# Fused sliding-window attention and MLP: four PSUM banks for up-projections that run alone, scores issued beside value products, w_out in 8 KB runs

## The chip, the cores and the metric

The kernel runs on one core of a Trainium2 chip. The metric is the device time of one execution in microseconds. Three executions of the kernel before took 350.82, 351.66 and 353.08 us, so the median is 351.66 us.

## The reference

```python
def _attn_ref(q, k, v):                    # (8, 8, 576, 64) each: batch, heads, tokens, width
    scores = np.matmul(q, k.transpose(0, 1, 3, 2)) / 8
    rel = pos[:, None] - pos[None, :]
    scores = np.where((rel >= 0) & (rel < 64), scores, -1e9)
    ...                                    # softmax over the last axis
    return np.matmul(attn, v)

def _moe_ref(x, w_in, w_out):              # x: 4608 x 512, w_in: 512 x 2048, w_out: 2048 x 512
    h = x @ w_in
    g = h * (1.0 / (1.0 + np.exp(-1.702 * h)))
    return g @ w_out
```

Attention looks back 64 tokens. Its output, with the heads side by side, is the input of the MLP. The kernel computes in bf16 and adds up in fp32.

## The kernel before, in words

The 4608 tokens are cut in two ways. Attention goes by blocks m = 0 to 35 of 128 tokens; the MLP goes by chunks of 512 tokens, ch = 0 to 8, four blocks to a chunk.

One attention block is a line of small steps. `turn_pe` (L166) transposes q and k on TensorE into `qkt`; VectorE copies q out, ScalarE copies k out. Later batches are transposed by DMA instead (`turn_dma`, L110, on SP's queue). `scores` (L187) is 16 small matmuls into one PSUM tile; `exp` (L202, ScalarE) and `mask` (L206, VectorE) make the weights; `pv` (L215) is 16 small matmuls with the values; `norm` (L231, VectorE) divides. The result `xs` is transposed into `xT`, by TensorE and a ScalarE copy (`x_mm`, L253, `x_out`, L261) for the first three chunks, and by DMA (`x_dma`, L264) after that.

`up` (L271) makes one piece of the hidden layer: 16 matmuls of 128 moving columns, or 8 of 256, or 4 of 512, into one PSUM bank, then tanh on ScalarE (`th`) and one VectorE operation to `gT`. `down` (L292) is 4 matmuls of 512 columns into an output bank; four of them make 128 tokens of output, which `down_out` (L306) scales on ScalarE and ScalarE's own queue stores. So a chunk is 16 `up` pieces of equal work and 16 `down` pieces.

PSUM is eight banks: two for S (one tile of two banks), two for the tag T (one tile of two banks: the value products, or a transpose), two single banks for H (hidden pieces), two single banks for O (outputs, or transposes).

The order of work on every engine is the order of the program text; nothing is reordered. It has five stages:

1. Start, up to L342. Blocks 0 to 2 of batch 0 go through attention one after the other. `arrive` (L320) casts what has landed: q on VectorE, k on ScalarE, v on GpSimd. `warm` is idle matmuls of 512 columns. The weights are loaded from GpSimd's queue (`load_w_in`, `load_w_out`). At L345 a one-element GpSimd copy reads a part of w_out that is loaded third and writes the stage buffer that the next load takes: so SP's later loads start only when that part has landed.
2. Up-projection of chunk 0, L349 to L363: 16 calls of `up`, alone on TensorE but for block 3.
3. Down-projection of chunk 0, L366 to L386, with block 4 in between (L369 to L381).
4. Up-projection of chunk 1, L391 to L412: four rounds, each with one attention block (m + 1) and four calls of `up`.
5. From L461: slots 16 ch + i. Every slot is one `up` of chunk ch and one `down` of chunk ch - 1. Attention steps are hung into the slots by tables: `pe` between the two, `post` ahead of the slot. There `scores(m)` stands in slot `slot_s[m]`, its exp one slot later, mask and `pv(m)` two slots later.

Of the kernel before, what the change touches and what calls it, by code (L numbers as in the profile page):

```python
# [1 line left out]

# [26 lines left out]
def kernel(  # L29
# [14 lines left out]
    xs_pool = ctx.enter_context(tc.tile_pool(name="xs", bufs=3))  # L44
    rc_pool = ctx.enter_context(tc.tile_pool(name="rc", bufs=2))
    xt_pool = ctx.enter_context(tc.tile_pool(name="xt", bufs=2))
    th_pool = ctx.enter_context(tc.tile_pool(name="th", bufs=2))
    gt_pool = ctx.enter_context(tc.tile_pool(name="gt", bufs=8))
    ob_pool = ctx.enter_context(tc.tile_pool(name="ob", bufs=4))
    psS = ctx.enter_context(tc.tile_pool(name="psS", bufs=1, space=bass.MemoryType.PSUM))  # L50
# [67 lines left out]
    def load_w_in(j):  # L118
        f = slice(512 * j, 512 * j + 512)
        nc.gpsimd.dma_start(  # L120
            out=w_in_sb[:, :, f], in_=moe_w_in.rearrange("(c p) f -> p c f", p=P)[:, :, f]
        )

    def load_w_out(j):
        f = slice(4 * j, 4 * j + 4)
        nc.gpsimd.dma_start(
            out=w_out_sb[:, f, :], in_=moe_w_out.rearrange("(c p) d -> p c d", p=P)[:, f, :]
        )


# [35 lines left out]
    def turn_pe(pool, tag, b, i):  # L166
        n = size(i)
        ps = pool.tile([P, 8, P], bf16, name="turn", tag=tag)
        for w in range(2):
            for hp in range(4):  # L170
                nc.tensor.transpose(  # L171
                    out=ps[:, 4 * w + hp, 0:n],
                    in_=rows[b % 2][w][0:n, i, P * hp : P * hp + P],
                    identity=ident[0:n, 0:n],
                )
        for w, op in enumerate((nc.vector.tensor_copy, nc.scalar.copy)):
            op(  # L177
                out=qkt[b % 2][:, w::2, PAD + P * i : PAD + P * i + n],
                in_=ps[:, 4 * w : 4 * w + 4, 0:n],
            )  # L180
# [20 lines left out]

    def exp(m):  # L202
        E_of[m] = ep_pool.tile([P, 2, 512], bf16, name="E", tag="E")
        nc.scalar.activation(out=E_of[m][:], in_=S_of.pop(m)[:], func=AF.Exp, scale=scale)  # L204

    def mask(m):  # L206
        z = next((t for t, b, j in blocks_of(m) if j == 0), None)
        pt = PT_of[m] = ep_pool.tile([P, 2, 512], bf16, name="PT", tag="PT")
        nc.vector.tensor_tensor(  # L209
            out=pt[:].rearrange("p a f -> p (a f)"),  # L210
            in0=E_of.pop(m)[:].rearrange("p a f -> p (a f)"),
            in1=masks[z][:].rearrange("p a t g c -> p (a t g c)"),
            op=ALU.mult,
        )
# [31 lines left out]
    def x_dst(m):  # L246
        ch = m // 4
        if m % 4 == 0:
            how = "pe" if ch < 3 else "dma"
            xT[ch] = xt_pool.tile([P, 4, 512], bf16, name=f"xT_{how}", tag=f"xT_{how}")  # L250
        return xT[ch][:, :, (m % 4) * P : (m % 4) * P + P]

# [13 lines left out]


    gT = {}
    H_of, O_of = {}, {}

    def up(ch, f, nf, t0, nt):  # L271

        ps = psH.tile([P, nf, nt], fp32, name="hps", tag="H")
        for g in range(nf):
            for c in range(4):
                nc.tensor.matmul(  # L276
                    ps[:, g, :],
                    lhsT=w_in_sb[:, c, (f + g) * P : (f + g + 1) * P],
                    rhs=xT[ch][:, c, t0 : t0 + nt],
                    start=(c == 0),  # L280
                    stop=(c == 3),
                )
        th = th_pool.tile([P, nf, nt], bf16, name="th", tag="th")
        nc.scalar.activation(out=th[:], in_=ps[:], func=AF.Tanh, scale=0.851)  # L284
        if (ch, f // 4) not in gT:
            gT[ch, f // 4] = gt_pool.tile([P, 4, 512], bf16, name="gT", tag="gT")
        nc.vector.scalar_tensor_tensor(  # L287
            out=gT[ch, f // 4][:, f % 4 : f % 4 + nf, t0 : t0 + nt],
            in0=th[:], scalar=1.0, in1=ps[:], op0=ALU.add, op1=ALU.mult,
        )  # L290

    def down(ch, i):  # L292

# [12 lines left out]
    def down_out(ch, tsub):  # L306
        o_sb = ob_pool.tile([P, DM], fp32, name="o_sb", tag="o_sb")
        nc.scalar.activation(out=o_sb[:], in_=O_of.pop((ch, tsub))[:], func=AF.Copy, scale=0.5)  # L308
        nc.scalar.dma_start(out=out_tiled[:, ch * 4 + tsub, :], in_=o_sb[:])

    def warm(n):
        ps = psH.tile([P, 512], fp32, name="idle", tag="H")
# [14 lines left out]
    exp(0)  # L327
    for m in range(3):
        arrive(0, m + 1)
        if m == 1:  # L330
            for j in range(4):
                load_w_in(j)
        mask(m)
        pv(m)
        norm(m)
        turn_pe(psO, "O", 0, m + 1)
        x_mm(m, psO, "O")
        x_out(m)
        scores(m + 1)
        exp(m + 1)  # L340
        if m < 2:
            warm(4)  # L342
    for j in range(4):
        load_w_out(j)
    nc.gpsimd.tensor_copy(out=stage[5][0:1, 0, 0:1], in_=w_out_sb[0:1, 8, 0:1])  # L345
    load_f32(0, 4)
    for i in range(5):
        load_f32(1, i)
    up(0, 0, 4, 0, P)  # L349
    up(0, 0, 4, P, P)  # L350
    mask(3)
    pv(3)
    norm(3)
    up(0, 0, 4, 2 * P, P)
    up(0, 4, 4, 0, P)
    x_mm(3, psO, "O")
    x_out(3)
    up(0, 4, 4, P, P)
    up(0, 4, 4, 2 * P, P)
    up(0, 0, 4, 3 * P, P)  # L360
    up(0, 4, 4, 3 * P, P)
    for f in range(8, 16):
        up(0, f, 1, 0, 512)  # L363


    for i in range(16):  # L366
        if i % 4 == 0 and i > 0:
            down_out(0, i // 4 - 1)
        if i == 10:  # L369
            arrive(0, 4)  # L370
            arrive(1, 0)
            turn_pe(psH, "H", 0, 4)
            turn_pe(psH, "H", 1, 0)
# [12 lines left out]
    down_out(0, 3)  # L386


    b2 = iter([lambda i=i: load_f32(2, i) for i in range(5)])
    next(b2)()  # L390
    for m in range(4, 8):  # L391
        scores(m + 1)
        exp(m + 1)
        t0 = (m % 4) * P
        up(1, 0, 4, t0, P)
        up(1, 4, 4, t0, P)
        mask(m + 1)
        pv(m + 1)
        norm(m + 1)
        if m < 7:  # L400
            arrive(1, m - 2)
        next(b2)()
        if m >= 6:
            cast_qk(2, m - 6, (nc.gpsimd, nc.gpsimd))
            turn_dma(2, m - 6)
            cast_v(2, m - 6)
        up(1, 8, 4, t0, P)
        x_mm(m + 1, psO, "O")
        x_out(m + 1)
        if m < 7:  # L410
            turn_pe(psO, "O", 1, m - 2)
        up(1, 12, 4, t0, P)  # L412

# [8 lines left out]
    def later(slot, g):  # L424
        post.setdefault(slot, []).append(g)

    slot_s = {9: 32, 10: 36, 11: 40, 12: 43, 13: 46}
    for m in range(14, NM):
        slot_s[m] = max(slot_s[m - 1] + 3, 4 * (m - 4) - 2)
    slot_pv = {m: s + 2 for m, s in slot_s.items()}  # L430

    for m in range(9, NM):
        if m < 12:
            at(slot_pv[m] + 1, lambda m=m: x_mm(m, psT, "T"), [lambda m=m: x_out(m)])
    for m in range(9, NM):
        at(slot_s[m], lambda m=m: scores(m), [lambda m=m: exp(m)])
        later(slot_pv[m], lambda m=m: mask(m))
        at(slot_pv[m], lambda m=m: pv(m), [lambda m=m: norm(m)])
        if m >= 12:
            later(slot_pv[m] + 1, lambda m=m: x_dma(m))  # L440

    for i in range(2, 5):
        at(32 + 2 * (i - 2), lambda i=i: cast_qk(2, i, (nc.gpsimd, nc.gpsimd)))
        at(32 + 2 * (i - 2), lambda i=i: turn_dma(2, i))
        at(32 + 2 * (i - 2), lambda i=i: cast_v(2, i))
    for b in range(3, B):
        free = slot_pv.get((9 * (b - 1) - 1) // 2, 31) + 2
        for i in range(5):
            use = slot_s[(S * b + P * i) // P]
            at(max(free, 38) + i, lambda b=b, i=i: load_bf16(b, i))  # L450
            at(use - 5, lambda b=b, i=i: turn_dma(b, i))
            at(use - 5, lambda b=b, i=i: shift_v(b, i))

    def unit(ch, i):
        if ch < 4:
# [54 lines left out]
```

## Time and profile before

| | |
|---|---|
| median of three runs | 351.66 us |
| the profiled execution | 355.03 us, of which the span is 353.3 us |
| TensorE | 310.0 us busy, 88% of the span |
| VectorE, ScalarE, GpSimd | 46%, 45%, 38% |
| DMA | mean 124 GB/s; in tenths by 40 slices 9999899946499999799999999993343331110021 |
| granted TensorE clock | mean 0.985 |

The profile shows the profiled execution alone. [...] The idle time beside a record is the engine's idle time before it and what ended it.

### The profile page before, as it was taken

To read this page: it belongs to the slowest core of one execution; us is meant where nothing else is said; L and a number is where in the kernel's file an instruction comes from. 1 tells how busy PE (TensorE), PEld (TensorE's weight loads), DVE (VectorE), ACT (ScalarE), POOL (GpSimd) and SP (SyncE) were. 2 spreads that over 40 slices of the span, in tenths; PEclk is the share of its full clock that TensorE was granted. 3 is DMA by queue.
4 is the path that set the end of the run, shared out by engine and by line. 5 is a ranking of instruction groups with operands and counts; after the bars stand their busy time and mean duration, and the time that the engine had idled before them with its cause. 6 is when DMAs were issued, how large, how long until landed. Compare 5 with 4: busy or idle time off the path is not lost.

```text
span 353.3 us, 7859 instructions
## 1 busy us (share of the span) xinstructions
PE 310.0 (88%) x3240; PEld 187.1 (53%) x3240; DVE 163.4 (46%) x285; ACT 158.0 (45%) x249; POOL 133.5 (38%) x190
## 2 busy tenths in 40 slices
PE   2777897677789996999999999999999999999995
PEld 1447343466666664676665665665444444444442
DVE  4535531456554453545445545544545544533400
ACT  3463424555444443444454454444445444444421
POOL 3670043745398589234983923492000000000000
PEclk9998999998899999999999999999999999999999
DMA  9999899946499999799999999993343331110021
GB/s 171 187 182 204 153 202 243 237 95 121 84 121 139 148 158 135 80 132 168 148 117 163 185 148 143 126 113 77 87 94 87 79 76 45 46 59 31 32 75 73
DMA packets 164579, 43.83 MB, mean 124 GB/s; under 512 B 155840, under 2 KB 159936, under 8 KB 164544
## 3 DMA queue, kind: packets, MB, share of 16 engines
q0 software_dynamic: 74544, 13.05, 53.5%
q1 hardware_dynamic: 84816, 20.85, 36.0%
q10 hardware_dynamic: 5184, 9.44, 7.4%
q8 instruction: 25, 0.41, 0.5%
q14 instruction: 10, 0.08, 0.1%
HBM read 36.70 MB, written 9.44 MB: 131 GB/s over the span
## 4 chain that ended last, share of the span: by engine, by line
PE 60%; DVE 17%; ACT 12%; DMA 6%; issue 2%; ACTq 1%; SPq 0%
PE ops L298 26%; PE hps L276 26%; DVE gT L287 8%; ACT th L284 7%; DVE PT L209 6%; PE Tacc L223 4%; DMA xT_dma<-xs 4%; PE S L194 3%; DMA stage<-in_k_dram 3%; ACT E L204 2%; DVE xs L236 2%; ACT o_sb L308 1%; ACT qkt L177 1%; PE turn L171 1%; DVE qkt L177 1%
## 5 line engine op out<-in xcount | busy, mean ns | idle before, releaser
L287 DVE SCALAR_TENSOR_TENSOR gT<-th,hps 128x512 bf16<-128x512 bf16 x144 | 98.9, 687 | 142.4 <-ACT th L284 142.0
L284 ACT ACTIVATE th<-hps 128x512 bf16<-128x512 f32 x144 | 85.9, 597 | 143.2 <-PE hps L276 131.1
L298 PE MATMUL ops<-w_out_sb,gT 128*128 128x512 bf16 x576 | 143.8, 380 | 0.0
L276 PEld LDWEIGHTS <-w_in_sb 128*128 128x128 bf16 x1376 | 102.9, 100 | 51.9 <-issue 6.0
L276 PE MATMUL hps<-xT_dma,w_in_sb 128*128 128x128 bf16 (+2 forms) x704 | 99.4, 282 | 3.1 <-DMA xT_dma<-xs 3.1
L298 PEld LDWEIGHTS <-gT 128*128 128x128 bf16 x576 | 51.2, 98 | 51.5
L276 PE MATMUL hps<-xT_pe,w_in_sb 128*128 128x128 bf16 (+1 forms) x672 | 52.9, 235 | 2.4 <-DVE gT L287 2.1
L102 POOL DMA_DIRECT2D v_nat<-in_v_dram x25 | 21.5, 860 | 43.7 <-issue 42.5
L204 ACT ACTIVATE E<-S 128x1024 bf16<-128x1024 f32 x36 | 36.7, 1020 | 2.1 <-PE S L194 1.6
L308 ACT ACTIVATE o_sb<-ops 128x512 f32<-128x512 f32 x36 | 21.5, 598 | 25.5 <-PE ops L298 25.4
L223 PEld LDWEIGHTS <-PT 128*64 128x64 bf16 x576 | 12.6, 114 | 33.5 <-DVE PT L209 33.4
L223 PE MATMUL Tacc<-v_nat,PT 128*64 128x65 bf16 x256 | 14.8, 202 | 12.5 <-DVE PT L209 12.5
L236 DVE TENSOR_TENSOR xs<-Tacc,rc 128x512 bf16<-128x512 f32 x36 | 24.9, 691 | 1.2
L223 PE MATMUL Tacc<-v_off,PT 128*64 128x65 bf16 x320 | 16.6, 201 | 9.6 <-DVE PT L209 9.6
L209 DVE TENSOR_TENSOR PT<-E,mask_None 128x1024 bf16<-128x1024 bf16 x28 | 20.3, 725 | 4.2 <-ACT E L204 4.2
L101 POOL DMA_DIRECT2D rows_k<-in_k_dram x25 | 21.6, 863 | 0.0
L101 POOL DMA_DIRECT2D rows_q<-in_q_dram x25 | 21.4, 856 | 0.0
L86 POOL CAST v_off<-stage 64x512 bf16<-64x512 f32 x15 | 9.1, 610 | 26.7 <-DMA stage<-in_v_dram 26.6
L194 PE MATMUL S<-qkt 64*128 64x64 bf16 x576 | 16.0, 196 | 3.6 <-ACT qkt L177 3.5
L106 POOL COPY v_off<-v_nat 64x528 bf16<-64x528 bf16 x25 | 16.8, 676 | 6.0 <-DMA v_nat<-in_v_dram 5.0
L194 PEld LDWEIGHTS <-qkt 64*128 64x128 bf16 x576 | 11.2, 98 | 12.0 <-issue 5.7
L108 POOL COPY v_off<-v_nat 64x528 bf16<-64x528 bf16 x20 | 13.7, 684 | 1.2
(39 smaller groups left out, 106.8 us busy)
## 6 DMA issues: line engine op xcount, KB each, us to landing
out_dram<-o_sb ACTq DMA_DIRECT2D x36, 256.0 KB, 2.5
stage<-in_q_dram SPq DMA_DIRECT2D x12, 256.0 KB, 5.1
stage<-in_k_dram SPq DMA_DIRECT2D x12, 256.0 KB, 5.1
stage<-in_v_dram SPq DMA_DIRECT2D x12, 256.0 KB, 5.2
rows_q<-in_q_dram POOLq DMA_DIRECT2D x20, 128.0 KB, 5.4
rows_k<-in_k_dram POOLq DMA_DIRECT2D x20, 128.0 KB, 6.0
v_nat<-in_v_dram POOLq DMA_DIRECT2D x20, 128.0 KB, 5.2
w_in_sb<-in_moe_w_in_dram POOLq DMA_DIRECT2D x4, 512.0 KB, 10.5
```

The costliest lines, as they stand in the source:

```text
L101: nc.gpsimd.dma_start(out=heads(rows[b % 2][w][0:n, i, :]), in_=rows_of(src, b, i))
L102: nc.gpsimd.dma_start(out=v_nat[b % 2][0:n, i, :, 0:D], in_=rows_of(v, b, i))
L194: nc.tensor.matmul(st[:, h % 2, t * 256 + hp * 64 : t * 256 + hp * 64 + 64], lhsT=src[part, 2 * hp + 1, 64 * j : 64 * j + 128], rhs=src[pa ...
L204: nc.scalar.activation(out=E_of[m][:], in_=S_of.pop(m)[:], func=AF.Exp, scale=scale)
L209: nc.vector.tensor_tensor(out=pt[:].rearrange("p a f -> p (a f)"), in0=E_of.pop(m)[:].rearrange("p a f -> p (a f)"), in1=masks[z][:].rearr ...
L223: nc.tensor.matmul(acc[t * 64 : t * 64 + 64, h // 4, (h % 4) * 66 : (h % 4) * 66 + 65], lhsT=pt[:, epos : epos + 64], rhs=win, start=True, ...
L236: nc.vector.tensor_tensor(out=xs[:].rearrange("p (b h d) -> p b h d", b=2, h=4), in0=view[:, :, :, 0:D], in1=rc[:].to_broadcast([P, 2, 4, D]),
L276: nc.tensor.matmul(ps[:, g, :], lhsT=w_in_sb[:, c, (f + g) * P : (f + g + 1) * P], rhs=xT[ch][:, c, t0 : t0 + nt], start=(c == 0), stop=(c ...
L284: nc.scalar.activation(out=th[:], in_=ps[:], func=AF.Tanh, scale=0.851)
L287: nc.vector.scalar_tensor_tensor(out=gT[ch, f // 4][:, f % 4 : f % 4 + nf, t0 : t0 + nt], in0=th[:], scalar=1.0, in1=ps[:], op0=ALU.add, o ...
L298: nc.tensor.matmul(O_of[ch, tsub][:, :], lhsT=gT[ch, j][:, f, tsub * P : (tsub + 1) * P], rhs=w_out_sb[:, 4 * j + f, :], start=(j == 0 and ...
L308: nc.scalar.activation(out=o_sb[:], in_=O_of.pop((ch, tsub))[:], func=AF.Copy, scale=0.5)
```

## The change

The diff does these things.

- `up` is split into its matmuls, its tanh and its VectorE step. With `wide=True` every second piece takes a bank of O in place of one of H. Stages 2 and 4 use this.
- The loops of stages 1 to 4 are put in another order. In stage 1 the transposes of the next block stand ahead of mask and pv, the idle matmuls are dealt in twos, and six stand ahead of stage 2. In stage 4 a round begins with the transposes, and `scores` follows the first piece.
- Chunk 0 and 1 store their outputs from SP's queue. Blocks 1 to 4 of batch 1 are cast by GpSimd alone. Chunk 3 gets `xT` through TensorE. The first quarter of w_in is loaded one block earlier.
- In stage 5, `scores(m+1)` stands in the slot of `pv(m)`; exp follows one slot later, mask two, and `pv(m+1)` at least three slots later, but for block 9. The slots of `pv` from block 9 on stay as they were. The later batches' loads are spread over three slots each, and `x_dma` stands one slot later.
- w_out is read so that a partition takes four neighbouring rows of 2 KB. That deals the features to partitions in fours, and `up` takes its weights with a step of four columns to match.

```diff
-    th_pool = ctx.enter_context(tc.tile_pool(name="th", bufs=2))
+    th_pool = ctx.enter_context(tc.tile_pool(name="th", bufs=3))
...
-            out=w_out_sb[:, f, :], in_=moe_w_out.rearrange("(c p) d -> p c d", p=P)[:, f, :]
+            out=w_out_sb[:, f, :],
+            in_=moe_w_out[512 * j : 512 * j + 512, :].rearrange("(p c) d -> p c d", c=4),
...
-            how = "pe" if ch < 3 else "dma"
+            how = "pe" if ch < 4 else "dma"
...
-    def up(ch, f, nf, t0, nt):
-        ps = psH.tile([P, nf, nt], fp32, name="hps", tag="H")
+    def up_mm(ch, f, nf, t0, nt, wide=False):
+        pool, tag = (psO, "O") if wide and next(turns) % 2 else (psH, "H")
+        ps = pool.tile([P, nf, nt], fp32, name="hps", tag=tag)
+        f0 = 512 * (f // 4)
...
-                    lhsT=w_in_sb[:, c, (f + g) * P : (f + g + 1) * P],
+                    lhsT=w_in_sb[:, c, f0 + (f + g) % 4 : f0 + 512 : 4],
...
+    def up(*args, **kw):
+        up_g(*up_th(*up_mm(*args, **kw)))
...
-        nc.scalar.dma_start(out=out_tiled[:, ch * 4 + tsub, :], in_=o_sb[:])
+        eng = nc.sync if ch < 2 else nc.scalar
+        eng.dma_start(out=out_tiled[:, ch * 4 + tsub, :], in_=o_sb[:])
...
+    GG = (nc.gpsimd, nc.gpsimd)
...
     for m in range(3):
         arrive(0, m + 1)
-        if m == 1:
-            for j in range(4):
+        if m == 0:
+            load_w_in(0)
+        elif m == 1:
+            for j in range(1, 4):
                 load_w_in(j)
+        turn_pe(psO, "O", 0, m + 1)
         mask(m)
         pv(m)
         norm(m)
-        turn_pe(psO, "O", 0, m + 1)
+        warm(2)
+        scores(m + 1)
+        exp(m + 1)
+        warm(2)
         x_mm(m, psO, "O")
         x_out(m)
-        scores(m + 1)
-        exp(m + 1)
-        if m < 2:
-            warm(4)
...
-    up(0, 0, 4, 0, P)
-    up(0, 0, 4, P, P)
+    warm(6)
     mask(3)
+    up(0, 0, 4, 0, P, wide=True)
     pv(3)
     norm(3)
...
-        if i == 10:
+        if i == 9:
             arrive(0, 4)
             arrive(1, 0)
...
-            arrive(1, 1)
+            arrive(1, 1, GG)
         down(0, i)
+        if i == 14:
+            x_mm(4, psT, "T")
+            x_out(4)
...
     for m in range(4, 8):
+        t0 = (m % 4) * P
+        turn_pe(psT, "T", 1, m - 3)
+        u = up_mm(1, 0, 4, t0, P, wide=True)
         scores(m + 1)
+        u = up_th(*u)
         exp(m + 1)
-        t0 = (m % 4) * P
-        up(1, 0, 4, t0, P)
-        up(1, 4, 4, t0, P)
+        up_g(*u)
+        u = [up_mm(1, f, 4, t0, P, wide=True) for f in (4, 8)]
+        u = [up_th(*x) for x in u]
         mask(m + 1)
         pv(m + 1)
+        up_g(*u[0])
         norm(m + 1)
+        up_g(*u[1])
         if m < 7:
-            arrive(1, m - 2)
+            arrive(1, m - 2, GG)
...
-        up(1, 8, 4, t0, P)
-        x_mm(m + 1, psO, "O")
+        up(1, 12, 4, t0, P, wide=True)
+        x_mm(m + 1, psT, "T")
         x_out(m + 1)
-        if m < 7:
-            turn_pe(psO, "O", 1, m - 2)
-        up(1, 12, 4, t0, P)
...
-    slot_s = {9: 32, 10: 36, 11: 40, 12: 43, 13: 46}
...
+    slot_pv = {8: 32, 9: 34, 10: 38, 11: 42, 12: 45}
+    for m in range(13, NM):
+        slot_pv[m] = max(slot_pv[m - 1] + 3, 4 * (m - 4) - 2)
+    for m in range(8, NM):
+        s = slot_pv[m]
+        if m + 1 < NM:
+            at(s, lambda m=m: scores(m + 1), [lambda m=m: exp(m + 1)])
+            later(s + 2, lambda m=m: mask(m + 1))
+        if m > 8:
+            at(s, lambda m=m: pv(m), [lambda m=m: norm(m)])
+            if m < 16:
+                at(s + 1, lambda m=m: x_mm(m, psT, "T"), [lambda m=m: x_out(m)])
+            else:
+                later(s + 2, lambda m=m: x_dma(m))
...
-            use = slot_s[(S * b + P * i) // P]
-            at(max(free, 38) + i, lambda b=b, i=i: load_bf16(b, i))
-            at(use - 5, lambda b=b, i=i: turn_dma(b, i))
+            use = slot_pv[(S * b + P * i) // P - 1]
+            come = max(free, 36) + 3 * i
+            at(come, lambda b=b, i=i: load_bf16(b, i))
+            at(max(use - 5, come + 4), lambda b=b, i=i: turn_dma(b, i))
```

## Rows read from the trace of the kernel before

**Rows 1.** Busy time by stage: busy us (x instructions) per engine, then clock, DMA share, GB/s.
```profile
0.00:24.13 24.13, 13.23 (x164) 7.80 (x165) 11.22 (x30) 10.20 (x15) 15.03 (x29) 1.00 1.08 177
24.13:46.19 22.06, 17.97 (x186) 12.58 (x181) 11.28 (x18) 10.46 (x18) 1.73 (x4) 0.92 1.07 186
46.19:64.38 18.19, 16.12 (x113) 7.50 (x112) 4.51 (x10) 6.07 (x10) 7.44 (x12) 1.00 1.09 218
64.38:100.39 36.01, 25.78 (x438) 22.23 (x436) 19.60 (x34) 19.01 (x33) 20.05 (x31) 0.91 0.66 125
100.39:138.90 38.51, 33.70 (x476) 23.92 (x476) 18.92 (x30) 18.42 (x29) 31.66 (x41) 1.00 1.84 142
138.90:353.30 214.40, 203.16 (x1872) 113.09 (x1872) 97.81 (x164) 93.84 (x146) 57.59 (x76) 1.00 0.84 100
```
**Rows 2.** Groups of instructions by line and shape: busy us, mean ns of one, idle before.
```profile
L276 PEld LDWEIGHTS <-w_in_sb 128*128 128x128 bf16 x1376 | 102.9, 100 | 51.9 <-issue 6.0 <-DMA xT_dma<-xs 3.2 <-DVE gT L287 0.2
L276 PE MATMUL hps<-xT_pe,w_in_sb 128*128 128x128 bf16 x640 | 44.8, 228 | 0.8 <-DVE gT L287 0.4
L204 ACT ACTIVATE E<-S 128x1024 bf16<-128x1024 f32 x36 | 36.7, 1020 | 2.1 <-PE S L194 1.6 <-ACT o_sb L308 0.4
L236 DVE TENSOR_TENSOR xs<-Tacc,rc 128x512 bf16<-128x512 f32 x36 | 24.9, 691 | 1.2
L209 DVE TENSOR_TENSOR PT<-E,mask_None 128x1024 bf16<-128x1024 bf16 x28 | 20.3, 725 | 4.2 <-ACT E L204 4.2
L276 PE MATMUL hps<-xT_dma,w_in_sb 128*128 128x128 bf16 x256 | 16.9, 219 | 2.7 <-DMA xT_dma<-xs 2.7
L177 ACT COPY qkt<-turn 128x512 bf16<-128x512 bf16 x8 | 4.7, 586 | 11.0 <-DVE qkt L177 11.0
L177 DVE COPY qkt<-turn 128x512 bf16<-128x512 bf16 x8 | 3.4, 422 | 4.9 <-PE turn L171 4.9
```
**Rows 3.** Timeline of TensorE, weight loads and matmuls: start us, us, what, idle before.
```profile
101.38 0.29 PEld L194 LDWEIGHTS <-qkt 64*128 64x128 bf16 x16
102.60 1.06 PE L276 MATMUL hps<-xT_pe,w_in_sb 128*128 128x128 bf16 x16
103.49 1.03 PE L298 MATMUL ops<-w_out_sb,gT 128*128 128x512 bf16 x4
```
**Rows 4.** Timeline of ScalarE in the start stage, columns as in Rows 3.
```profile
19.17 1.02 ACT L204 ACTIVATE E<-S 128x1024 bf16<-128x1024 f32 x1 [0.28 <-PE S L194]
20.09 0.61 ACT L95 CAST rows_k<-stage 128x512 bf16<-128x512 f32 x1
...
24.30 1.02 ACT L204 ACTIVATE E<-S 128x1024 bf16<-128x1024 f32 x1
```
**Rows 5.** Timeline of TensorE in the up-projection of chunk 0.
```profile
39.48 2.01 PE L276 MATMUL hps<-xT_pe,w_in_sb 128*128 128x512 bf16 x8 [0.41 <-DVE gT L287]
```
**Rows 6.** Timeline of ScalarE, its queue, and TensorE in the down-projection of chunk 0.
```profile
53.30 0.60 ACT L308 ACTIVATE o_sb<-ops 128x512 f32<-128x512 f32 x1 [2.85 <-PE ops L298]
56.16 0.34 ACTq L309 DMA_DIRECT2D out_dram<-o_sb  x1
...
57.21 0.29 PE L171 MATMUL turn<-ident,rows_k 64*128 64x64 bf16 x4 [2.00 <-ACT rows_k L95]
```
**Rows 7.** Timeline of GpSimd: the one-element copy behind the third w_out load.
```profile
39.35 0.18 POOL L345 CAST stage<-w_out_sb 1x1 f32<-1x1 bf16 x1 [14.89 <-DMA w_out_sb<-in_moe_w_out_dram]
```
**Rows 8.** Waits of TensorE from 64.38 to 100.39: total us, times, longest.
```profile
PE Tacc L223 <- DVE PT L209: 8.7, 4, 2.3
```
**Rows 9.** Waits of TensorE from 100.39 to the end: total us, times, longest.
```profile
PE Tacc L223 <- DVE PT L209: 9.0, 26, 0.8
PE hps L276 <- DMA xT_dma<-xs: 3.1, 2, 2.7
```
**Rows 10.** Timeline of TensorE where a value product waits for its mask.
```profile
104.36 1.06 PE L276 MATMUL hps<-xT_pe,w_in_sb 128*128 128x128 bf16 x16
106.00 0.22 PE L223 MATMUL Tacc<-v_off,PT 128*64 128x65 bf16 x1 [0.59 <-DVE PT L209]
```

More of the change, by code (lines that the diff above doesn't have):

```diff
@@ L1 @@
+import itertools
 from contextlib import ExitStack
@@ L268 @@
     gT = {}
-    H_of, O_of = {}, {}
-    def up(ch, f, nf, t0, nt):
-        ps = psH.tile([P, nf, nt], fp32, name="hps", tag="H")
+    O_of = {}
+    turns = itertools.count()
+    def up_mm(ch, f, nf, t0, nt, wide=False):
+        pool, tag = (psO, "O") if wide and next(turns) % 2 else (psH, "H")
+        ps = pool.tile([P, nf, nt], fp32, name="hps", tag=tag)
+        f0 = 512 * (f // 4)
         for g in range(nf):
@@ L282, in up, with up_th, up_g @@
                 )
+        return ps, ch, f, nf, t0, nt
+    def up_th(ps, ch, f, nf, t0, nt):
         th = th_pool.tile([P, nf, nt], bf16, name="th", tag="th")
         nc.scalar.activation(out=th[:], in_=ps[:], func=AF.Tanh, scale=0.851)
+        return th, ps, ch, f, nf, t0, nt
+    def up_g(th, ps, ch, f, nf, t0, nt):
         if (ch, f // 4) not in gT:
@@ L348 @@
         load_f32(1, i)
-    up(0, 0, 4, 0, P)
-    up(0, 0, 4, P, P)
+    warm(6)
     mask(3)
+    up(0, 0, 4, 0, P, wide=True)
     pv(3)
     norm(3)
-    up(0, 0, 4, 2 * P, P)
-    up(0, 4, 4, 0, P)
-    x_mm(3, psO, "O")
+    up(0, 0, 4, P, P, wide=True)
+    up(0, 0, 4, 2 * P, P, wide=True)
+    x_mm(3, psT, "T")
     x_out(3)
[L358 to L361, printed above, removed]
+    up(0, 4, 4, 0, P, wide=True)
+    up(0, 4, 4, P, P, wide=True)
+    up(0, 0, 4, 3 * P, P, wide=True)
+    up(0, 4, 4, 2 * P, P, wide=True)
+    up(0, 4, 4, 3 * P, P, wide=True)
     for f in range(8, 16):
-        up(0, f, 1, 0, 512)
+        up(0, f, 1, 0, 512, wide=True)
     for i in range(16):
@@ L373 @@
             turn_pe(psH, "H", 1, 0)
-        if i == 11:
+        if i == 10:
             scores(4)
@@ L380 @@
             norm(4)
-            arrive(1, 1)
+            arrive(1, 1, GG)
         down(0, i)
-    x_mm(4, psH, "H")
-    x_out(4)
-    turn_pe(psH, "H", 1, 1)
+        if i == 14:
+            x_mm(4, psT, "T")
+            x_out(4)
     down_out(0, 3)
-    b2 = iter([lambda i=i: load_f32(2, i) for i in range(5)])
-    next(b2)()
     for m in range(4, 8):
+        t0 = (m % 4) * P
+        turn_pe(psT, "T", 1, m - 3)
+        u = up_mm(1, 0, 4, t0, P, wide=True)
         scores(m + 1)
+        u = up_th(*u)
         exp(m + 1)
-        t0 = (m % 4) * P
-        up(1, 0, 4, t0, P)
-        up(1, 4, 4, t0, P)
+        up_g(*u)
+        u = [up_mm(1, f, 4, t0, P, wide=True) for f in (4, 8)]
+        u = [up_th(*x) for x in u]
         mask(m + 1)
         pv(m + 1)
+        up_g(*u[0])
         norm(m + 1)
+        up_g(*u[1])
         if m < 7:
-            arrive(1, m - 2)
-        next(b2)()
+            arrive(1, m - 2, GG)
+        load_f32(2, m - 4)
         if m >= 6:
-            cast_qk(2, m - 6, (nc.gpsimd, nc.gpsimd))
+            cast_qk(2, m - 6, GG)
             turn_dma(2, m - 6)
             cast_v(2, m - 6)
-        up(1, 8, 4, t0, P)
-        x_mm(m + 1, psO, "O")
+        up(1, 12, 4, t0, P, wide=True)
+        x_mm(m + 1, psT, "T")
         x_out(m + 1)
-        if m < 7:
-            turn_pe(psO, "O", 1, m - 2)
-        up(1, 12, 4, t0, P)
     pe = {}
@@ L425, in later @@
         post.setdefault(slot, []).append(g)
-    slot_s = {9: 32, 10: 36, 11: 40, 12: 43, 13: 46}
[L428 to L440, printed above, removed]
+    slot_pv = {8: 32, 9: 34, 10: 38, 11: 42, 12: 45}
[12 more added lines that the diff above has]
+                later(s + 2, lambda m=m: x_dma(m))
+    at(32, lambda: load_f32(2, 4))
     for i in range(2, 5):
-        at(32 + 2 * (i - 2), lambda i=i: cast_qk(2, i, (nc.gpsimd, nc.gpsimd)))
-        at(32 + 2 * (i - 2), lambda i=i: turn_dma(2, i))
-        at(32 + 2 * (i - 2), lambda i=i: cast_v(2, i))
+        at(4 * i + 24, lambda i=i: cast_qk(2, i, GG))
+        at(4 * i + 24, lambda i=i: turn_dma(2, i))
+        at(4 * i + 24, lambda i=i: cast_v(2, i))
     for b in range(3, B):
@@ L448 @@
         for i in range(5):
-            use = slot_s[(S * b + P * i) // P]
-            at(max(free, 38) + i, lambda b=b, i=i: load_bf16(b, i))
-            at(use - 5, lambda b=b, i=i: turn_dma(b, i))
-            at(use - 5, lambda b=b, i=i: shift_v(b, i))
+            use = slot_pv[(S * b + P * i) // P - 1]
+            come = max(free, 36) + 3 * i
+            at(come, lambda b=b, i=i: load_bf16(b, i))
+            at(max(use - 5, come + 4), lambda b=b, i=i: turn_dma(b, i))
+            at(max(use - 5, come + 4), lambda b=b, i=i: shift_v(b, i))
     def unit(ch, i):
```

## The prediction, on record before the result

> **What bounds the kernel now.** I read the page's shares first (TensorE 88% busy), then the table by stage, then the waits of TensorE in each stage. The table [rows 1] cuts the span at the first matmul of each stage: start, up of chunk 0, down of chunk 0, up of chunk 1, and the merged slots in two pieces. In the merged stage TensorE is busy 237 of 253 us; ahead of it, 73 of 100 us. So the kernel is bound by TensorE's order of work: its matmuls, and the places where it waits for a short chain on other engines. DMA is full until 64 us (shares 1.07 to 1.09 in the first three stages) and not after; ScalarE and VectorE are nowhere over 55%.
>
> A piece, `up` or `down`, costs TensorE 0.87 to 0.89 us at full clock: 0.89 from a start of `up` to the next `down` [rows 3], 16 matmuls at a pitch of 55.6 ns. [...]
>
> **Start and up of chunk 0 (0 to 46.19 us).** Before, one round of the start lasts 24.30 - 19.17 = 5.13 us from exp to exp [rows 4]. In the new order the key cast still stands behind exp on ScalarE (20.09, just as exp ends), the transposes behind the cast, and now mask waits on VectorE behind the copy that waits for those transposes. My chain for a round: exp 1.02, `x_out` 0.59 (now between exp and the cast), cast 0.61, key transposes 0.45, copy 0.42, mask 0.73, pv 0.55, two idle matmuls 0.86, scores 0.5, the sum 5.73, and some 0.08 for each of seven handoffs: 6.3 us. (Durations: [rows 2, 4]; the matmul steps are estimates from the pitch at half clock.) So the start gets slower, by some 1.1 us in each of two rounds. The last scores end near 26.6 instead of 24.1; then eight idle matmuls (some 0.22 each) and a transpose bring the first `up` to 28.5. From there 16 pieces at 0.89, plus 0.4 for pv, 0.2 for the transpose and 0.4 for the handover to the output banks, are 15.2 us. Before, the stage took 22.06: pairs of pieces wait 0.41 for a bank [rows 5], pv waits for mask, and the clock is at 0.92. Four banks end the first: ScalarE and VectorE are busy 10.5 and 11.3 us in the stage [rows 1], at most 0.7 us a piece, which fits within 0.89, and a bank has four pieces' time to come free. The stage ends at 43.8 to 44 instead of 46.19: **-2.2 us**. Bounds: -5 if the new start is no slower than the old, +2 if every handoff costs double and the clock starts low.
>
> **Down of chunk 0 (18.19 us).** ScalarE finishes an output at 53.90 and gets its store off at 56.16; only then come the key casts, and TensorE stands 2.00 us [rows 6]. With the stores on SP's queue ScalarE is free for the casts, and they stand one piece earlier. On SP each store waits for its ScalarE copy; behind it are loads and transposes of batch 2, which nobody needs for over 10 us. New: 16 pieces at 0.87, transposes 0.9, scores, pv and `x_mm` 1.0, and 0.3 of switches: 16.1 us, **-2.1 us**. What hides the rest: the third w_out part lands at 39.35 [rows 7], so the fourth should be there by 43 and is needed near 46.5; batch 1's first tile is needed at 52. If this cover is gone, the loads pace the stage and the gain is nothing. The longer runs of w_out I cost at nothing, as the wait for them ends ahead of their use; the bound is one or two us either way.
>
> **Up of chunk 1 (36.01 us).** Here pv waits 8.7 us in four rounds [rows 8], and a round is 9.0 us for 3.6 us of `up`. In the new order a round is still one chain, since T has one buffer, passed from transposes to pv to `x_mm`: transposes 0.45, copies 0.42 and 0.59 one after the other, scores 0.35, exp 1.02, mask 0.73, pv 0.40, norm 0.69, `x_mm` 0.22, `x_out` 0.59 [rows 2], the matmul steps by the pitch. That is 5.46, with handoffs and norm's short reciprocal 1.3 more: 6.8 us. The four `up` pieces lie beside it, two of them under exp and mask. Four rounds are 27.2; I add 1.0 for stretches at the lower clock, as this stage shows 0.91 now. So 28.2 instead of 36.0: **-7.8 us**. GpSimd takes eight casts of some 0.6 us more, as long as ScalarE's of the same shape [rows 4]; two tiles of five casts are at most 6 us of work in a round of 6.8, so it stays under the chain. The moved casts cost TensorE nothing then; if GpSimd fell behind, a round would become 7 to 8 us. Bounds: -12 (rounds of 6), -3 (rounds of 8).
>
> **Merged slots (252.9 us).** pv waits 9.0 us for its mask, 26 times [rows 9]. A wait of 0.59 delays pv by 104.36 + 0.89 to 106.00, that is 0.75 [rows 10], so up to 0.16 more than the idle shown; I take half, 2.1 in all. With mask two slots behind scores and pv a third slot later, a slot (1.74 us) lies between mask and its use. Only block 9 keeps the old distance. Chunk 3's transpose by DMA was late by 2.7 us; by TensorE it is there in time, for four times 0.22. The other wait of that kind (0.4) may grow by 0.6, since the slots before it get shorter and the DMA does not. So -9.0 - 2.1 - 2.7 + 0.9 + 0.6 + 0.4 (block 9): **-11.9 us**. Late next: norm ahead of `x_mm`, some tenths three times. Bounds: -15 (the switch between shapes is also saved, once per block), -7 (transposes of later batches, whose loads now start later, arrive late twice). The third `th` buffer and the spread loads I cost at nothing; the slack of ScalarE and the DMA share of 0.84 hide them, and without that cover they are in these bounds.
>
> **The strided weights** belong to all 1376 loads of `up`. No row of before has one. The nearest rows: loads of 128 contiguous columns stand 98 ns in the records, but 16 of them start within 0.29 - 0.10 us, one per 13 ns, or 26 ns for each of the two row groups [rows 3]. A piece of 128 columns needs one per 55.6 ns, so a load may take twice as long and cost nothing. Lower end: 0 (a stride cannot make it faster). Upper end: loads that don't overlap at all follow at their mean of 100 ns [rows 2]; 640 + 256 matmuls of 128 columns are then 44 ns later each: +39.8 us. Pieces of 256 and 512 columns hide 100 ns. I take 0, the row of 26 ns being of the same operation.
>
> [...]
>
> **The sum.** -2.2 - 2.1 - 7.8 - 11.9 = -24.0 us from the profiled execution's 355.03: 331.0. That execution is 1.0% above the median of 351.66, so I scale by 351.66 / 355.03: **328 us**.
>
> **Rivals.**
> (a) *The strided load sets the pitch of the 128-column pieces.* For it: no such load in the trace, and the loads of w_in are back to back with the matmuls. Against: the 26 ns. It decides from 55.6 + 24.0 / 896 = 82 ns per load; at 100 ns the time is 328 + 39 = 367 us, slower than before. At 70 to 80 ns it would eat most of the gain. 13%, most of it slower.
> (b) *The first 64 us are paced by DMA.* For it: shares over 1.0, and the same bytes. Against: TensorE waits there name casts and banks, not loads. Then the 4.3 us of the first two stages are lost: 332 us. 12%.
> (c) *The stage of chunk 1 keeps its length*, because its chain gets new waits (T's one buffer, GpSimd's casts) or TensorE falls to the lower clock in the gaps. For it: the stage shows 0.91 now. Against: 8.7 us of its waits have one cause that is moved. 328 + 7.8 = 336 us. 13%.
> (d) *The merged slots get nothing*: the wait for mask turns into one for the next transpose. 340 us. 6%.
>
> **How the numbers follow.** My forecast has 56%, and its own range is 319 to 336. The best ends of the four stages (-5, -3, -12, -15) give 317; the worst (+2, 0, -3, -7) give 343, which also holds (b), (c) and (d). I take 317 to 345; outside are (a) and a little beyond. A measurement of this kernel can tell about 1% from no change. Faster by more than that: all but (a) and a pile of worst ends, 83%; within: 6%; slower: 11%.
>
> **What would show it.** Right: pv no longer waits for mask after the first merged slots; a round of stage four lasts about 6.8 us; up pieces of chunk 0 follow at 0.89 us; 16 matmuls of 128 columns still take 0.89 us from `up` to the next piece. Wrong: a longer pitch there (a); a first `up` well ahead of or behind 28.5 us; TensorE waiting for `rows` or `qkt` in the stage of chunk 1; waits for `xT_dma` or `qkt` of several us in the merged slots.

## The result, and the profile after

The changed kernel takes 327.95 us in the median of four runs (327.28 to 329.68), the kernel before 352.37 us beside it: a ratio of 0.9328, with a 95% interval of 0.9267 to 0.939. The forecast was 328. In the profiled executions the span falls from 353.3 to 326.8 us, by 26.5 us.

The table of the changed kernel by the same five stages: the start, up of chunk 0, down of chunk 0, up of chunk 1, merged slots (busy us and instructions of PE, PEld, DVE, ACT and POOL, then clock, DMA share, GB/s). The clock of 1.00 in its first line is not what the start ran at: its last idle matmuls follow at 0.43 us, where those of the two-bank kernel follow at 0.22.

```profile
0.00:30.89 30.89, 17.25 (x172) 9.56 (x175) 11.69 (x31) 11.63 (x16) 14.29 (x29) 1.00 1.16 200
30.89:45.88 14.99, 14.94 (x181) 11.46 (x180) 10.39 (x17) 9.43 (x16) 2.56 (x5) 1.00 1.02 193
45.88:62.31 16.43, 16.06 (x115) 7.71 (x116) 4.74 (x9) 5.97 (x10) 12.72 (x21) 1.00 0.86 187
62.31:88.34 26.03, 22.71 (x434) 20.05 (x432) 17.96 (x32) 17.46 (x29) 16.17 (x24) 1.00 0.89 176
88.34:326.80 238.46, 228.51 (x2330) 146.22 (x2363) 116.40 (x194) 114.19 (x178) 89.73 (x121) 1.00 1.06 112
```

Set against [rows 1], the start lasts 6.8 us longer (30.89 against 24.13) and each later stage is shorter: 14.99 against 22.06, 16.43 against 18.19, 26.03 against 36.01, 238.46 against 252.91.

The start, on ScalarE: the exps of blocks 1 to 3, and the key cast that now stands ahead of the transposes.

```profile
14.25 1.02 ACT L206 ACTIVATE E<-S 128x1024 bf16<-128x1024 f32 x1 [2.59 <-PE S L196]
20.78 1.02 ACT L206 ACTIVATE E<-S 128x1024 bf16<-128x1024 f32 x1 [2.30 <-PE S L196]
22.59 0.62 ACT L96 CAST rows_k<-stage 128x512 bf16<-128x512 f32 x1
27.24 1.02 ACT L206 ACTIVATE E<-S 128x1024 bf16<-128x1024 f32 x1 [2.29 <-PE S L196]
```

A round is 6.5 us, where [rows 4] has 5.13. TensorE after it: the last four idle matmuls, then the pieces of chunk 0, and two rounds of chunk 1.

```profile
29.18 1.91 PE L330 MATMUL idle<-mask_None,ident 128*128 128x512 bf16 x4 [0.22 <-issue]
34.51 11.54 PE L281 MATMUL hps<-xT_pe,w_in_sb 128*128 128x128 bf16 x111
53.74 0.29 PE L173 MATMUL turn<-ident,rows_q 64*128 64x64 bf16 x4
54.14 0.29 PE L173 MATMUL turn<-ident,rows_k 64*128 64x64 bf16 x4
68.83 0.38 PE L173 MATMUL turn<-ident,rows_q 128*128 128x128 bf16 x4 [0.72 <-ACT xT_pe L264]
75.34 0.38 PE L173 MATMUL turn<-ident,rows_q 128*128 128x128 bf16 x4 [0.72 <-ACT xT_pe L264]
```

The pieces of chunk 0 run through with no wait for a bank [rows 5], and the 2.00 us ahead of the key transposes [rows 6] are gone. A round of chunk 1 lasts 75.34 - 68.83 = 6.51 us; what is left of waiting is the 0.72 for `x_out`, which holds T's one buffer, and once 0.2 for mask. TensorE's waits in the merged slots, and one slot in which scores and value products stand side by side:

```profile
PE ops L312 <- issue: 4.3, 27, 0.2
PE S L196 <- DMA qkt<-rows_k: 1.0, 1, 1.0
PE hps L281 <- ACT xT_pe L264: 0.7, 1, 0.7
...
100.60 1.06 PE L281 MATMUL hps<-xT_pe,w_in_sb 128*128 128x128 bf16 x16
101.59 0.41 PE L196 MATMUL S<-qkt 64*128 64x64 bf16 x16
101.93 0.22 PE L225 MATMUL Tacc<-v_off,PT 128*64 128x65 bf16 x1
```

Both waits of [rows 9] are gone. (The 27 short ones are no waits: each stands where the record of the first of four `down` matmuls is missing.)

### The profile page after: what moved, and what is told of

It reads as the page before. It is cut to its first block, busy times and chain, and to the rows that moved or that the text cites. A ratio compares the mean times of both kernels' runs of the same rounds, so it can differ in the third digit from the quotient of the medians.

```text
span 326.8 us, 7852 instructions
## 1 busy us (share of the span) xinstructions
PE 299.5 (92%) x3226; PEld 195.0 (60%) x3266; DVE 161.2 (49%) x281; ACT 158.7 (49%) x249; POOL 135.5 (41%) x198
## 4 chain that ended last, share of the span: by engine, by line
PE 87%; ACT 5%; DMA 3%; issue 2%; DVE 2%; SPq 0%; ACTq 0%
PE hps L281 38%; PE ops L312 36%; PE Tacc L225 4%; PE S L196 4%; DMA qkt<-rows_k 2%; PE idle L330 2%; PE turn L173 2%; ACT xT_pe L264 1%; DMA stage<-in_k_dram 1%; ACT th L292 1%; PE pxt L259 1%; DVE PT L211 1%; ACT rows_k L96 1%; DVE qkt L179 1%; ACT E L206 1%
## 5 line engine op out<-in xcount | busy, mean ns | idle before, releaser
L312 PE MATMUL ops<-w_out_sb,gT 128*128 128x512 bf16 x542 | 136.7, 379 | 4.8 <-issue 4.5
L281 PEld LDWEIGHTS <-w_in_sb 128*128 128x128 bf16 x1376 | 108.0, 114 | 39.9 <-issue 2.4
L312 PEld LDWEIGHTS <-gT 128*128 128x128 bf16 x576 | 53.0, 98 | 51.2
L281 PE MATMUL hps<-xT_dma,w_in_sb 128*128 128x256 bf16 (+1 forms) x446 | 82.2, 318 | 0.1
L281 PE MATMUL hps<-xT_pe,w_in_sb 128*128 128x128 bf16 (+1 forms) x927 | 64.9, 225 | 1.0 <-ACT xT_pe L264 0.7
L107 POOL COPY v_off<-v_nat 64x528 bf16<-64x528 bf16 x25 | 16.3, 656 | 10.1 <-DMA v_nat<-in_v_dram 8.2
L179 DVE COPY qkt<-turn 128x512 bf16<-128x512 bf16 (+1 forms) x10 | 4.0, 398 | 21.2 <-PE turn L173 21.2
```

Source lines behind the costliest of these rows:

```text
L281: nc.tensor.matmul(ps[:, g, :], lhsT=w_in_sb[:, c, f0 + (f + g) % 4 : f0 + 512 : 4], rhs=xT[ch][:, c, t0 : t0 + nt], start=(c == 0), stop= ...
L312: nc.tensor.matmul(O_of[ch, tsub][:, :], lhsT=gT[ch, j][:, f, tsub * P : (tsub + 1) * P], rhs=w_out_sb[:, 4 * j + f, :], start=(j == 0 and ...
```

## The experiments

Profiled executions of one start differ by up to 1.8 us in when exp of block 3 comes (25.56 to 27.35 us in seven kernels that share the start, the changed one at 27.24), and TensorE's pace differs too: the six idle matmuls ahead of the first `up` piece follow at 0.22 us in the two-bank kernel and at 0.43 in the changed one. Their first piece comes between 27.94 and 30.97 us. So beside each time I give, where it matters, the length from the first `up` piece to the end of the span: 326.8 - 30.89 = 295.9 us for the changed kernel. The kernel before was run again beside each set of runs, with medians from 352.13 to 355.21 us, so ratios of different sets can differ by 1% where the times are equal; between experiments I compare the times.

**Contiguous weights, 2 KB runs.**

```diff
-                    lhsT=w_in_sb[:, c, f0 + (f + g) % 4 : f0 + 512 : 4],
+                    lhsT=w_in_sb[:, c, (f + g) * P : (f + g + 1) * P],
...
-            in_=moe_w_out[512 * j : 512 * j + 512, :].rearrange("(p c) d -> p c d", c=4),
+            in_=moe_w_out.rearrange("(c p) d -> p c d", p=P)[:, f, :],
```

> The changed kernel with contiguous weight columns for the up-projections again, and w_out read in 2 KB runs as before. Theory: the step of four columns is free, because a weight load has room to take twice as long, and the third w_out part landed 35.65 us into the changed kernel, ten microseconds ahead of the first down piece. So the time stays within 1 us of 328, 16 matmuls of 128 columns keep their 0.89 us, and only the landing of that part moves, to about 38 or 39 us. Rival: the step costs something in every piece that the sum of the stages hides; then this kernel is faster, at 5 ns per load of the 896 short pieces by 4.5 us, and the 0.89 us becomes shorter.

327.45 us, ratio to before 0.925 [0.9193, 0.9306]; 325.5 - 29.09 = 296.4 us from the first piece, half a microsecond more than with the stride. The stride costs nothing that the times show. One part of the expectation missed: the third w_out part lands at the same time, by GpSimd's copy behind it, the first row the changed kernel's, the second this one's.

```profile
35.65 0.18 POOL L363 CAST stage<-w_out_sb 1x1 f32<-1x1 bf16 x1 [11.90 <-DMA w_out_sb<-in_moe_w_out_dram]
```
```profile
35.71 0.18 POOL L363 CAST stage<-w_out_sb 1x1 f32<-1x1 bf16 x1 [11.24 <-DMA w_out_sb<-in_moe_w_out_dram]
```

So the longer runs don't bring it forward from 39.35 [rows 7]. Nor does the new order of the start: with the old order, further down, it lands at 35.49. What is left is the first quarter of w_in, asked for at 12.42 instead of 16.07: from 15 to 20 us the DMA engines moved 119 GB/s before and 206 after. No run moves that load alone, so this cause is found by elimination. Before first, then after:

```profile
15.00:20.00 5.00, 4.18 (x48) 2.51 (x48) 2.30 (x5) 2.07 (x4) 4.83 (x8) 1.00 0.83 119
```
```profile
15.00:20.00 5.00, 3.12 (x31) 1.75 (x29) 1.75 (x4) 1.96 (x4) 3.33 (x6) 1.00 1.22 206
```

**The price of a stride by itself.** Extra matmuls between the up and the down pieces of chunk 0.

```diff
+    def probe(pool, tag, step, n, cols):
+        ...
+                lhsT=w_in_sb[:, r % 4, o : o + 128 * step : step],
+                rhs=ident[:, 0:cols],
+    for st in (1, 2, 4, 8, 16):
+        probe(psH, "H", st, 32, 32)
+    for st in (1, 4):
+        probe(psH, "H", st, 32, 128)
```

> The changed kernel with seven groups of 32 extra matmuls between the up- and the down-projections of chunk 0, whose results nobody reads: 32 moving columns and weights of 128 columns of w_in at a step of 1, 2, 4, 8 and 16 columns, then 128 moving columns at a step of 1 and 4. With 32 moving columns the pitch is set by the weight load, which the contiguous loads of the scores put at 26 ns per row group or less. Theory: at a step of four the load takes no more than 55 ns, so that 128 moving columns hide it and both groups with 128 run at 55 to 56 ns a matmul; with 32 columns the pitch at step 1 is 25 to 30 ns and at step 4 between that and 52. Rival: the step costs more than 55 ns a load and the up pieces are slower for it: then the last group runs at 60 ns or more. [...]

From the starts of the matmuls in the trace, the first and last of a group apart by 31 pitches:

| moving columns, step | 32, 1 | 32, 2 | 32, 4 | 32, 8 | 32, 16 | 128, 4 |
|---|---|---|---|---|---|---|
| ns per matmul | 25.1 | 25.0 | 33.4 | 62.1 | 62.3 | 55.8 |

(Of the matmuls with 128 columns at step 1 the first two thirds followed at 107 ns, with the granted clock at 0.50, and the rest at 56, with the clock at 1.00.) Busy time in short windows shows the same: the matmuls in flight in 0.4 us (for TensorE and its weight loads) at steps 2, 4, 8, then at the end of step 16 with the clock at 0.50, then 128 columns at step 1 with the clock at 0.50 and at step 4:

```profile
46.60:47.00 0.40, 0.40 (x23) 0.40 (x20) 1.00 1.11 243
48.20:48.60 0.40, 0.40 (x17) 0.40 (x15) 1.00 0.93 211
49.80:50.20 0.40, 0.40 (x10) 0.40 (x9) 1.00 1.23 263
52.20:52.60 0.40, 0.40 (x10) 0.40 (x9) 0.50 0.67 143
53.80:54.20 0.40, 0.40 (x6) 0.40 (x5) 0.50 0.89 204
55.80:56.20 0.40, 0.40 (x11) 0.40 (x9) 1.00 0.95 216
```

A pitch is that of a load with its matmul, so it bounds the load's price; at steps 1 and 2, where it is the same, the matmul may be what sets it. A load at step 4 takes at most 33 ns and hides under 55.8; at step 8 it would take 62, and by my estimate the 896 matmuls of 128 columns would pay about 6 ns each, 5.6 us. Against steps 1 and 2, step 4 costs 8 ns more and step 8 37 more; the cause is not shown.

**Mask close to its use.** Only the slots of scores, exp and mask are put back.

```diff
-        if m + 1 < NM:
-            at(s, lambda m=m: scores(m + 1), [lambda m=m: exp(m + 1)])
-            later(s + 2, lambda m=m: mask(m + 1))
         if m > 8:
+            at(s - 2, lambda m=m: scores(m), [lambda m=m: exp(m)])
+            later(s, lambda m=m: mask(m))
```

> The changed kernel with the old distances in the merged slots: scores and exp two slots ahead of the value products, mask in the same slot as they. Theory: TensorE waits for mask some 25 times again, 8.5 to 9 us of idle and about 2 us more beside it: 338 to 340. Rival: the waits are slack that other delays would have taken anyway, and the gain of the merged slots came from chunk 3's transposes and the spread loads: 330 to 333.

339.66 us, 0.9585 [0.9519, 0.9651]. The merged slots last 339.2 - 89.06 = 250.1 us, 11.7 more. TensorE's waits there:

```profile
PE Tacc L225 <- DVE PT L211: 8.5, 27, 0.8
```

So 8.5 us of idle cost 11.7: 0.12 per wait lies beside it, or the shared slot saves a switch that is lost here; no run tells the two apart. The trace of the changed kernel speaks for the switch: in chunk 1 value products that wait for nothing start 0.16 us after the last matmul ahead of them started, where matmuls of one kind follow at 0.056. By my estimate 27 such steps are 2.9 of the 3.2 us.

**Chunk 3 through the DMA again.**

```diff
-            how = "pe" if ch < 4 else "dma"
+            how = "pe" if ch < 3 else "dma"
...
-            if m < 16:
+            if m < 12:
...
-                later(s + 2, lambda m=m: x_dma(m))
+                later(s + 1, lambda m=m: x_dma(m))
```

> The changed kernel with chunk 3's transposes by DMA again, ordered as before the change. Theory: block 12's transpose lands late for the first up piece of chunk 3 by 2 to 3 us, as before; TensorE saves 0.9 us of transposes: the merged slots get 1.5 to 2.5 us longer, 330. Rival: with the loads spread over three slots each the DMA queues are free at that time and it lands sooner: 327 to 328.

331.67 us in one run; merged slots 330.0 - 87.03 = 243.0 us, 4.5 more. The wait for `xT` is as before, and a second wait for batch 3's transposes comes with it, in the same queue. The two waits are 3.9 us more than in the changed kernel. The gain of this part was sized too small, but the 4.5 are not chunk 3's alone: the edit also puts the DMA transposes of all later chunks one slot earlier.

```profile
PE hps L281 <- DMA xT_dma<-xs: 2.6, 1, 2.6
PE S L196 <- DMA qkt<-rows_k: 2.3, 2, 1.2
```

**Two banks.**

```diff
-        pool, tag = (psO, "O") if wide and next(turns) % 2 else (psH, "H")
+        pool, tag = (psH, "H")
```

> The changed kernel with every up piece in the two banks of H. Theory: in the up-projection of chunk 0 each pair of pieces waits 0.4 us for a bank again, some 6 or 7 pairs: 2.5 to 3 us. In the up-projection of chunk 1 the second and third piece of a round lie under exp and mask and the bank of the first is free late; 0.5 to 1 us per round. In all 5 to 6 us slower, about 333. Rival: the new order alone makes the gain of chunk 1 and the chain hides the banks there; then only chunk 0 pays, about 331.

332.42 us, 0.94 [0.9334, 0.9467]; 329.7 - 27.94 = 301.8 us from the first piece, 5.9 more. The stage of chunk 0 takes 47.38 - 27.94 = 19.4 us instead of 15.0, with the old wait in each pair; a round of chunk 1 takes 6.6 to 7.1 instead of 6.5.

```profile
39.22 2.02 PE L281 MATMUL hps<-xT_pe,w_in_sb 128*128 128x512 bf16 x8 [0.41 <-DVE gT L298]
```

**Stores on ScalarE's queue.**

```diff
-        eng = nc.sync if ch < 2 else nc.scalar
+        eng = nc.scalar
```

> The changed kernel with all stores on ScalarE's queue, as before. Theory: in the down-projection of chunk 0 ScalarE stands again behind its stores for 1 to 2 us ahead of the key casts, and TensorE waits about 1.5 to 2 us there: 330. Rival: the earlier loads and the place one piece earlier have removed that wait already, or the store is off in time because SP issues less then: no change, 328.

328.25 us in one run; 295.7 us from the first piece. The rival holds: TensorE waits 0.63 us, not 2, and wins it back later. A store now leaves 0.03 us after its copy (53.53, copy from 52.91 to 53.51), where [rows 6] has 2.26. In the kernel before, a load that SP issued at 53.04 took 2.82 us to issue while that store waited; here SP is still issuing loads, but those around the store take 0.65 to 1.45 us. What held the two up in the kernel before is not shown. But the stores on SP's queue are not where the 2.00 us went.

```profile
53.53 0.34 ACTq L324 DMA_DIRECT2D out_dram<-o_sb  x1
54.59 0.29 PE L173 MATMUL turn<-ident,rows_k 64*128 64x64 bf16 x4 [0.63 <-ACT rows_k L96]
```

**The old start.** Transposes in their old places, four idle matmuls behind each block (the third too), the rest as changed.

```diff
-        turn_pe(psO, "O", 0, m + 1)
         mask(m)
         pv(m)
         norm(m)
-        warm(2)
+        turn_pe(psO, "O", 0, m + 1)
+        x_mm(m, psO, "O")
+        x_out(m)
         scores(m + 1)
         exp(m + 1)
-        warm(2)
-        x_mm(m, psO, "O")
-        x_out(m)
+        warm(4)
```

> The changed kernel with the start loop in the old order: transposes of the next block behind norm, four idle matmuls per block, the rest as changed. Theory: the new order made the start slower (exp of block 3 at 27.24 us instead of 24.30, rounds of 6.5 instead of 5.1 to 5.5), because mask now waits for the key cast, the transposes and their copy. With the old order exp of block 3 is back near 24.5 and the end follows by 2 to 3 us: about 325.5. Rival: the start is only where slack shows; the loads of w_in and w_out pace the first 46 us, and the up-projections begin or the down-projections stall so that the time stays at 328.

326.31 us, 0.9204 [0.9141, 0.9266]. In the profiled executions exp of block 3 comes at 23.87 and the first piece at 27.26, 3.6 us earlier, and the span is 3.2 us shorter. But the changed kernel's profiled start is one of the late ones, and the two medians differ by 1.6 us. So the new order of the start is a loss of one to two us, and it reaches the end. Part of what the old order gains is lost again to a wait for w_in:

```profile
28.19 1.00 PE L281 MATMUL hps<-xT_pe,w_in_sb 128*128 128x128 bf16 x15 [0.71 <-DMA w_in_sb<-in_moe_w_in_dram]
```

**Two faster starts.** One casts q and k on VectorE, so that the key cast no longer stands behind exp; the other casts the block after next ahead of exp. Both leave out the idle matmuls ahead of scores.

```diff
-        arrive(0, m + 1)
+        arrive(0, m + 1, (nc.vector, nc.vector))
...
-        warm(2)
         scores(m + 1)
```

> The changed kernel with q and k of blocks 1 to 3 both cast by VectorE in the start, and without the two idle matmuls ahead of scores. Theory: the round of the start is the chain exp, key cast, key transposes, copy, mask, pv, idle matmuls, scores; with the cast beside exp and the idle matmuls out it falls from 6.5 us to 4.3 to 4.6, exp of block 3 comes near 22 instead of 27.2, and the first up piece near 25.5 instead of 30.9 unless w_in is late; the end follows by 3 to 5 us: 323 to 325. Rival: DMA paces the first 46 us: w_in or block 3's rows come later than the faster chain wants them, or the down-projections wait for w_out, and the time stays at 326 to 328.

> The changed kernel with the casts of the block after next ahead of exp in the start (ScalarE still casts k), so that the next block's transposes are ready beside exp, and without the two idle matmuls ahead of scores. Theory: the chain from exp to exp is then exp, mask, pv, scores and handoffs, 3.1 to 4 us a round, as long as the rows have landed; the loads come one block per 3.6 us. Exp of block 3 comes at 20 to 22 us, the first up piece at 24 to 25.5, the end at 322 to 324. Rival: exp now waits for the rows of the block after next, which land late behind w_in, and the round stays above 5 us: 326 to 328.

327.81 and 327.89 us (ratios 0.9234 and 0.9247): the times of the changed kernel, though exp of block 3 comes at 21.61 and 22.68. The up pieces begin at 25.14 in the first of the two, and then stand for 2.30 us. The granted clock is 0.91 in the mean of that stage, and the 32 matmuls of the next two pieces take 3.17 us (1.98 in the old start):

```profile
25.14 0.22 PE L281 MATMUL hps<-xT_pe,w_in_sb 128*128 128x128 bf16 x1
27.67 1.10 PE L281 MATMUL hps<-xT_pe,w_in_sb 128*128 128x128 bf16 x15 [2.30 <-DMA w_in_sb<-in_moe_w_in_dram]
29.28 3.17 PE L281 MATMUL hps<-xT_pe,w_in_sb 128*128 128x128 bf16 x32
```

The second of the two waits 2.47 us at the same place. In the first, the first quarter of w_in was asked for at 12.36, and no quarter took over 10.4 us to land: it was there by 22.8. The last was asked for at 17.1 and can have landed as late as 27.5, just ahead of the end of the wait. Two kernels ask why the second matmul waits: the fast VectorE start with contiguous columns, and with the stride but a tile for each quarter.

```diff
-    w_in_sb = keep.tile([P, 4, DFF], bf16, name="w_in_sb")
+    w_in_sb = [keep.tile([P, 4, 512], bf16, name=f"w_in_sb{j}") for j in range(4)]
...
-                    lhsT=w_in_sb[:, c, f0 + (f + g) % 4 : f0 + 512 : 4],
+                    lhsT=w_in_sb[f // 4][:, c, (f + g) % 4 : 512 : 4],
```

> The faster start (q and k cast by VectorE, no idle matmuls ahead of scores) with contiguous weight columns and 2 KB runs. In the kernel with that start and strided columns the first matmul of the first up piece ran at 25.14 us, and the second waited until 27.67 for a load of w_in; all of w_in's first quarter was asked for at 12.4. Theory A: a strided slice of the one w_in tile is taken to touch the other quarters too, so the first piece waits for all four loads, the last issued near 18 us; with contiguous columns that wait is gone, the first up piece runs through at about 25, the clock stays up, and the end is near 322. Theory B: the first quarter itself lands only near 27.5; then the wait stays here and the time is 325 to 328 as with the stride.

> The faster start, strided columns and 8 KB runs, but w_in in four tiles, one for each load. Theory A (a piece waits for quarters that it does not read): the wait of 2.3 us at the second matmul goes, the stage ends 3 us earlier, the end is near 321 to 322. Theory B (the first quarter is late): nothing changes, 324 to 328.

321.5 us, 0.9147 [0.9112, 0.9183], and 321.19, 0.9143 [0.9089, 0.9196]. Neither waits; the first piece, of the contiguous and then of the split kernel:

```profile
23.84 1.06 PE L281 MATMUL hps<-xT_pe,w_in_sb 128*128 128x128 bf16 x16
```
```profile
24.00 1.06 PE L281 MATMUL hps<-xT_pe,w_in_sb 128*128 128x128 bf16 x16
```

From that piece to the end they take 295.9 and 295.7 us, as the changed kernel does: the gain is all in the start. So the wait belongs to the strided slice of the one tile: the program's own order made a piece wait for quarters that it does not read. In the changed kernel the slow start hides it; with the old start 0.71 of it shows. Last, without the six idle matmuls:

```diff
-    warm(6)
     mask(3)
```

> As the kernel with four w_in tiles, and without the six idle matmuls ahead of the first up piece. Theory: up pieces keep TensorE as busy as idle matmuls do, so the first starts near 23 us, when the first quarter has landed, and the end comes 1.5 to 2 us earlier, near 320. Rival: the clock is lower there without the idle matmuls, or w_out and batch 1's rows now come late for the down-projection: no gain.

320.8 us, 0.9119 [0.9073, 0.9165], the fastest. The first piece is at 22.66, the span 318.5, 1.2 us shorter than with them, and from the first piece it takes 295.8; the step between the two medians, 0.4 us, is within their spread (319.01 to 321.45 and 320.32 to 322.76).

## Why the prediction was right, point by point

That the time was right to the microsecond is in part luck. The profiled execution of the kernel before lay 1.0% above the median, and the forecast took 3.1 us off its sum of 331.0 for that. The profiled execution of the changed kernel took 328.51, only 0.2% above its median, so 331.0 was 2.5 us too slow for it, and the scaling covered that. The 2.5 us are the difference of the sums by stages, in spans:

| stage | forecast | measured |
|---|---|---|
| start and up of chunk 0 | -2.2 | 45.88 - 46.19 = -0.3 |
| down of chunk 0 | -2.1 | 16.43 - 18.19 = -1.8 |
| up of chunk 1 | -7.8 | 26.03 - 36.01 = -10.0 |
| merged slots | -11.9 | 238.46 - 252.91 = -14.5 |
| sum | -24.0 | -26.5 |

- **Start.** The mechanism held: mask waits behind key cast, transposes and copy, and the old order is faster, by 1.6 us in the medians. Two terms were too small in the profiled execution: a round is 6.5, not 6.3 us, and the eight idle matmuls were priced at 0.22 us each; the last four follow at 0.43. The first piece came at 30.89, not 28.5. In the other kernels with this start it came from 27.94 on, so 28.5 lies within their range, and the -0.3 is the stage near its slowest. The pieces then took 14.99 us, where 15.2 were forecast, and the two-bank kernel shows the cause.
- **Down of chunk 0.** The sum held, the reason did not: the store's queue is worth nothing here. Either the earlier loads took the wait away or the casts that stand one piece earlier did; no run tells these apart. The loads were earlier, by elimination, because of the first quarter of w_in, which the prediction did not price at all.
- **Up of chunk 1.** The chain was right; a round took 6.5 instead of 6.8, and the microsecond added for the lower clock was not needed: the clock's row says 1.00, not 0.91, and the record of 16 matmuls is 1.06 us there, as in [rows 3], where the next piece starts after 0.89.
- **Merged slots.** The waits for mask were right. What lies beside each wait was taken as half of 0.16; the 11.7 us of the close mask leave 0.12 a wait, between the half and the whole. Chunk 3's transposes, forecast at -1.8, are worth up to 4.5 when taken out of the changed kernel. Together these are 16.2 us, where 14.5 were measured. What went against them was a new wait of 1.0 for a transposed tile of batch 3, within the bounds of the transposes' lateness; 0.7 stays open. That wait falls into the first 40 us of the merged slots. The prediction called DMA full until 64 us "and not after", but [rows 1] shows a share of 1.84 there.
- **Stride.** Free, as taken, and rival (a) is out: 33 ns, with 82 as the point from which it would decide. Rival (b) is out too: no matmul of chunk 0's up- or down-projection waits for a load in the changed kernel. The wait for w_in in the start with VectorE's casts was for quarters that the piece did not read, and went with a tile for each.

## What to carry to other kernels

Where an engine's order is fixed, move a consumer far enough behind its chain that another piece of work lies between; here one slot of 1.7 us, with scores beside the value products, was worth 11.7 us over 27 blocks. Price an inserted step by everything that the new order puts ahead of the critical operation on each engine, idle matmuls included (here the last four at 0.43 us each, where 0.22 was priced). After speeding up one stage, look for what the slow stage had been hiding: here a wait of 2.30 us for parts of a tile that the waiting piece does not read, removed by giving each load its own tile.

## What the runs showed of the hardware that was not expected

The pitch of a weight load with a matmul of 32 columns follows the load's stride in steps: 25 ns at steps 1 and 2, 33 at 4, 62 at 8 and 16. At step 16 the clock fell to half on the way, and the pitch stayed at 62. In the probe the granted clock fell to 0.50 near 51.4 us and rose again near 54.8, although matmuls followed each other without a gap: those ahead of the fall had 32 moving columns at 62 ns, those ahead of the rise 128 columns. In the changed kernel's start the clock's row says 1.00 while the last idle matmuls of 512 columns follow at 0.43 us, twice the 0.22 of the two-bank kernel: the row of this execution says 1.00 from its first microsecond on, so for the start the pitch tells more than the row.
